# Softmax normalisation and transposes by whole query block, and the first gate/up products on 256 rows, in an attention and gated-MLP kernel

## The chip, the cores and the metric

The kernel runs on one core of one Trainium2 chip. The metric is the device time of one execution in microseconds (us); lower is better. The core has a matrix engine (TensorE, PE in the profile, whose weight loads are listed as PEld), a vector engine (VectorE, DVE), an engine for elementwise functions (ScalarE, ACT), GpSimd (POOL), and SyncE (SP), which here only issues DMAs. PSUM is the memory that PE writes to, SBUF the working memory. The engines run on their own and wait for each other by semaphores.

## The reference

`x` is 2048 rows of 512 in bf16. It is normalised by row; the result `xn` goes into a 32-head attention over given key and value caches and into a gated MLP, and the two meet in the output:

```
xn = (x - mean) / sqrt(var + 1e-5)
q  = (xn @ wq) as 32 heads of 128
p  = softmax(q k^T / sqrt(128))          # 2048 x 2048 for each head
s  = (p v, heads side by side) @ wo
h  = relu(xn @ W_gate) * (xn @ W_up)     # 1792 columns
g  = silu(h @ W_down)
out = x + s * g
```

## The kernel before

**Phases.** First comes a head (`head_ln`): layer norm of the first four 128-row tiles and their transposes. Then the MLP, in four query blocks of 512 rows (Q = 0 to 3): `emit_gate_up` computes 14 column chunks of 128 for gate and up, `emit_down` the down product. The layer norm of the later rows runs beside the first query block (`ln_task`), and their transposes are done by DMA. Then attention: 32 heads with 4 query blocks of 512 rows make 128 blocks. Then the last output tiles.

**Head.** Twelve dummy matmuls (L479) run on PE while the input loads. `ln_stats`, `ln_aggr` and `ln_coef` make mean and scale on DVE, with the square root on ACT. `ln_norm` applies them: tiles 0 and 1 on POOL, tiles 2 and 3 on DVE. `head_transpose` transposes each tile with four PE matmuls into the PSUM ring, and ACT (tiles 0 to 2) or DVE (tile 3) copies the result to `xnT`. When all four are copied, gate and up of chunk 0 begin on all 512 rows (L423, L427). The weights come in three pieces, of 2, 6 and 6 chunks; the first piece of `W_up` is loaded from ACT's queue, all others from SP's.

**Attention blocks.** A block has 8 pairs of key tiles. For each pair PE makes two score tiles of 128 keys by 512 queries (`emit_S_tile`, L583), ACT takes the exponential of both at once (L593) into one of six `PT` buffers, and three pairs later PE multiplies with the values (`emit_PV_tile`, L676): for each key tile four matmuls, one for each 128 queries, into `ps_acc`. That accumulator takes two PSUM banks with two 128-query column blocks (j) each. A value tile has a 129th column of constants, so that each column block also sums its exponentials. Score tiles and projections share a ring of three PSUM slots of two banks (`ring_acquire`).

**Between blocks.** When a block's last value product is done, DVE divides by the sums, bank by bank (`emit_norm_bank`): a reciprocal over the bank's two sums (L606), then one scaling of 128x128 for each of its column blocks (L613) into `Onorm`. The next block's first product into a bank waits for that bank's scalings. SP waits for each bank's scalings and then issues one DMA transpose per column block into `OT_store` (L628). At the first block of every group of four heads (16 blocks) DVE first waits until all transposes of the group before have landed, since the 16 `Onorm` buffers are used again.

**Filling work.** A written plan (`plan`) puts other matmuls between the last score tile of a block and the first value product of the next: the Q projection of the next head (`emit_qp`, four matmuls, L516, copied out by DVE at L527), and from block 17 on an output projection tile of the group before (`emit_oproj_tile`, L537, added up by DVE at L550). In blocks 1 to 16 there is the Q projection alone. In the last head there are no Q projections; the last output projections and the first output tiles (`emit_final_tile`, L710, L718, L723) are spread there. With group 6 DVE does two more operations per tile (`emit_base`, L562, L565).

**End.** The last block's two banks are transposed on PE (`emit_last_transposes`, `flush_last_transposes`), ACT copies them, and the last four output tiles follow; each is multiplied and added on DVE and stored by SP.

The order on each engine is the order of the program. SP's queue is in order too: a DMA behind a wait stays there until the wait ends.

## Time and profile before

| | |
|---|---|
| median of three runs | 1294.82 us (1294.73 to 1296.88) |
| profiled execution | 1294.82 us, of which the profile's span is 1293.0 us |
| PE busy | 1283.3 us, 99% |
| PE weight loads busy | 832.8 us, 64% |
| ACT busy | 1001.6 us, 77% |
| DVE busy | 442.7 us, 34% |
| granted TensorE clock | 1.00 |

A time before a row is its start in us from the span's start, then its duration. A group row gives the line, the engine, the operation, output and input tiles with partitions x elements, the count, then busy time and the mean in ns, then the idle time before it and what ended it. A row of the waits gives who waited for whom: total us, number, longest. Matmuls are pipelined, so their listed durations overlap; the distance of two starts is what one costs on PE.

### The profile page before, as it was taken

To read this page: it belongs to the slowest core of one execution; us is meant where nothing else is said; L and a number is where in the kernel's file an instruction comes from. 1 tells how busy PE (TensorE), PEld (TensorE's weight loads), DVE (VectorE), ACT (ScalarE), POOL (GpSimd) and SP (SyncE) were. 2 spreads that over 40 slices of the span, in tenths; PEclk is the share of its full clock that TensorE was granted. 3 is DMA by queue.
4 is the path that set the end of the run, shared out by engine and by line. 5 is a ranking of instruction groups with operands and counts; after the bars stand their busy time and mean duration, and the time that the engine had idled before them with its cause. 6 is when DMAs were issued, how large, how long until landed. Compare 5 with 4: busy or idle time off the path is not lost.

```text
span 1293.0 us, 27683 instructions
## 1 busy us (share of the span) xinstructions
PE 1283.3 (99%) x11968; PEld 832.8 (64%) x11968; DVE 442.7 (34%) x1190; ACT 1001.6 (77%) x1109; POOL 11.5 (1%) x23
## 2 busy tenths in 40 slices
PE   9999999999999999999999999999999999999998
PEld 4444466666666666666666666666666666666665
DVE  6333322223323323323323323323323323334456
ACT  3322399998888888888888888888888888888884
POOL 2000000000000000000000000000000000000000
PEclk9999999999999999999999999999999999999999
DMA  9500112222222322232211322222223312232202
GB/s 260 114 1 1 22 34 46 50 54 47 53 52 54 69 53 54 52 68 54 48 36 38 70 52 53 53 69 54 52 52 53 69 29 41 53 69 54 49 16 74
DMA packets 250999, 71.69 MB, mean 55 GB/s; under 512 B 237824, under 2 KB 250880, under 8 KB 250880
## 3 DMA queue, kind: packets, MB, share of 16 engines
q1 hardware_dynamic: 250064, 69.41, 25.3%
q8 instruction: 95, 1.56, 0.5%
q10 hardware_dynamic: 816, 0.52, 0.1%
q14 instruction: 24, 0.20, 0.0%
HBM read 32.77 MB, written 2.10 MB: 27 GB/s over the span
## 4 chain that ended last, share of the span: by engine, by line
PE 96%; DVE 3%; DMA 1%; issue 0%; SPq 0%; POOL 0%; ACT 0%; DVEq 0%
PE ps_acc L676 35%; PE ps_r L583 33%; PE ps_r L516 7%; PE ps_r L537 7%; PE ps_r L423 4%; PE ps_acc L460 4%; PE ps_r L427 4%; DVE Onorm L613 2%; PE ps_r L710 1%; DVE rz_sb L606 0%; DMA OT_store<-Onorm 0%; SPq L628 0%; DMA x_sb<-in_A_x_dram 0%; DVE stats L314 0%; POOL xn_sb L339 0%
## 5 line engine op out<-in xcount | busy, mean ns | idle before, releaser
L593 ACT ACTIVATE PT<-ps_r 128x1024 bf16<-128x1024 f32 x1024 | 952.5, 1053 | 173.4 <-PE ps_r L583 173.4
L676 PE MATMUL ps_acc<-V_sb,PT 128*128 128x129 bf16 x8192 | 779.8, 220 | 2.4 <-DVE Onorm L613 0.6
L676 PEld LDWEIGHTS ps_acc<-V_sb,PT 128*128 128x128 bf16 x8192 | 621.6, 98 | 246.8 <-DVE Onorm L613 5.5
L583 PE MATMUL ps_r<-QT_sb,KT_sb 128*128 128x512 bf16 x2048 | 754.1, 379 | 0.0
L606 DVE RECIPROCAL rz_sb<-ps_acc 128x2 f32<-128x2 f32 x256 | 42.3, 165 | 721.2 <-PE ps_acc L676 701.6
L583 PEld LDWEIGHTS ps_r<-QT_sb,KT_sb 128*128 128x128 bf16 x2048 | 194.9, 98 | 1.1 <-DVE QT_sb L527 0.4
L613 DVE TENSOR_SCALAR Onorm<-ps_acc,rz_sb 128x128 bf16<-128x128 f32 x512 | 156.2, 347 | 9.1
L516 PE MATMUL ps_r<-xnT,Wq_sb 128*128 128x512 bf16 x512 | 130.9, 379 | 0.0
L537 PE MATMUL ps_r<-Wo_sb,OT_store 128*128 128x512 bf16 x448 | 114.6, 379 | 0.0
L516 PEld LDWEIGHTS ps_r<-xnT,Wq_sb 128*128 128x128 bf16 x512 | 49.8, 97 | 60.7 <-ACT PT L593 27.1
L527 DVE CAST QT_sb<-ps_r 128x512 bf16<-128x512 f32 x128 | 87.2, 681 | 0.7 <-PE ps_r L516 0.7
L537 PEld LDWEIGHTS ps_r<-Wo_sb,OT_store 128*128 128x128 bf16 x448 | 43.8, 98 | 52.9 <-ACT PT L593 0.2
L433 ACT ACTIVATE gr_sb<-ps_r 128x512 bf16<-128x512 f32 x56 | 33.4, 596 | 54.3 <-PE ps_r L423 54.1
L550 DVE TENSOR_TENSOR s_acc<-s_acc,ps_r 128x512 f32<-128x512 f32 x96 | 65.9, 687 | 13.1 <-PE ps_r L537 1.0
L423 PE MATMUL ps_r<-xnT,Wg_sb 128*128 128x512 bf16 x224 | 57.5, 379 | 0.6 <-ACT xnT L357 0.6
L427 PE MATMUL ps_r<-xnT,Wu_sb 128*128 128x512 bf16 x224 | 57.5, 379 | 0.0
L439 DVE TENSOR_TENSOR hT<-gr_sb,ps_r 128x512 bf16<-128x512 bf16 x56 | 38.4, 686 | 47.8 <-PE ps_r L427 45.0
L460 PE MATMUL ps_acc<-Wd_sb,hT 128*128 128x512 bf16 x224 | 49.0, 379 | 0.0
L466 ACT ACTIVATE sig_sb<-ps_acc 128x512 f32<-128x512 f32 x16 | 9.6, 597 | 38.8 <-PE ps_acc L460 38.8
L423 PEld LDWEIGHTS ps_r<-xnT,Wg_sb 128*128 128x128 bf16 x224 | 21.9, 98 | 26.9 <-ACT xnT L357 0.7
L427 PEld LDWEIGHTS ps_r<-xnT,Wu_sb 128*128 128x128 bf16 x224 | 21.9, 98 | 26.4
L460 PEld LDWEIGHTS ps_acc<-Wd_sb,hT 128*128 128x128 bf16 x224 | 21.9, 98 | 26.4
(36 smaller groups left out, 126.8 us busy)
## 6 DMA issues: line engine op xcount, KB each, us to landing
V_sb<-in_A_v_cache_dram SPq DMA_DIRECT2D x32, 512.0 KB, 5.1
OT_store<-Onorm SPq DMA_TRANSPOSE x508, 2.4
Wq_sb<-in_A_wq_dram SPq DMA_DIRECT2D x32, 128.0 KB, 2.7
Wo_sb<-in_A_wo_dram SPq DMA_DIRECT2D x8, 512.0 KB, 4.2
Wd_sb<-in_B_W_down_dram SPq DMA_DIRECT2D x1, 1792.0 KB, 13.5
Wg_sb<-in_B_W_gate_dram SPq DMA_DIRECT2D x2, 768.0 KB, 9.0
Wu_sb<-in_B_W_up_dram SPq DMA_DIRECT2D x2, 768.0 KB, 10.0
x_sb<-in_A_x_dram SPq DMA_DIRECT2D x3, 512.0 KB, 10.8
```

Source lines behind the costliest of these rows:

```text
L423: ins = pe.matmul(ps_r[:, gb, :], Wg_sb[:, c, fs], xnT[:, c, qs], start=(c == 0), stop=(c == DC - 1))
L427: ins = pe.matmul(ps_r[:, gb + 1, :], Wu_sb[:, c, fs], xnT[:, c, qs], start=(c == 0), stop=(c == DC - 1))
L460: ins = pe.matmul(ps_acc[:, jb, 0:D], hT[par][:, fc, j * 128:(j + 1) * 128], Wd_sb[:, fc, :], start=(fc == 0), stop=(fc == FC - 1))
L516: ins = pe.matmul(ps_r[:, bank, :], Wq_sb[b][:, c, :], xnT[:, c, qs], start=(c == 0), stop=(c == DC - 1))
L527: etok = sem_qpe.sig(dve.tensor_copy(QT_sb[b][:, qs], ps_r[:, bank, :]))
L537: ins = pe.matmul(ps_r[:, bank, 0:D], OT_store[g % 2][:, hh, n * 128:(n + 1) * 128], Wo_sb[g % 2][:, hh, :], start=(hh == 0), stop=(hh == ...
L550: dve.tensor_tensor(s_acc[:, n, :], s_acc[:, n, :], ps_r[:, bank, 0:D], ALU.add)
L583: ins = pe.matmul(ps_r[:, 2 * s + tt, :], KT_sb[h % 2][:, t * 128:(t + 1) * 128], QT_sb[h % 2][:, qs], start=True, stop=True)
L593: act.activation(PT[pb][:], ps_r[:, 2 * s:2 * s + 2, :], ACTF.Exp, scale=scale)
L606: rztok = sem_rz.sig(dve.reciprocal(rz_sb[:, bank, :, :], z_ap))
L613: dve.tensor_scalar(Onorm[ob][:, j, :], ps_acc[:, bank, base:base + Dh], rz_sb[:, bank, jj, :], None, op0=ALU.mult,)
L676: ins = pe.matmul(o_ap, PT[pb][:, tt, j * 128:(j + 1) * 128], V_sb[vb][:, t, 0:VW], start=(t == 0 and j % 2 == 0), stop=(t == KT - 1 and j ...
```

## The change

1. **Normalisation by block.** `emit_norm_bank` becomes `emit_norm_block`: it waits for the whole block, then makes one reciprocal over the four sums and one multiplication of 128x512 with the reciprocals broadcast along each column block. Both accumulator banks are free when that is done. The last block keeps a two-step form, `emit_norm_last`, one multiplication of 128x256 for each half.
2. **One DMA transpose per block**, of 128x512, in place of four of 128x128. `Onorm` has 20 buffers in place of 16, and DVE's wait for the transposes of the group before moves from the group's first block to its fifth.
3. **Head.** Tiles 0 and 1 are normalised on DVE. The transposes go to the accumulator's banks in place of the ring. Gate and up of the first three chunks are made in two halves of 256 rows: the first half of chunks 0 and 1 after tiles 0 and 1, with three dummy matmuls before it; then the transposes of tiles 2 and 3, the first half of chunk 2, and the second halves. The weights come in pieces of 3, 5 and 6 chunks, and all of them from SP's queue. What follows a chunk's products is put in a function, `finish_gate_up`, and is unchanged.

The change's name also speaks of value rows at an even stride. The value tiles have a row stride of 136 elements (`VS = Dh + 8`) in both kernels, and the diff doesn't touch it.

```diff
-    NON = G * QB
+    NON = G * QB + 4
...
-    TPG = 16 * 4 * G * QB
+    TPG = 16 * G * QB
...
-                FCS = [0, min(2, FC), min(8, FC), FC]
+                FCS = [0, min(3, FC), min(8, FC), FC]
+                HFC = 3
...
-                load_w(act, Wu_sb, wu_src, sem_wu, 0)
+                load_w(sp, Wu_sb, wu_src, sem_wu, 0)
...
                 def head_transpose(n, ntok, eng, sem):
-                    tp_ps = ps_r[:, n, :].bitcast(BF16)
+                    tp_ps = acc_bf[n % 2]
+                    _wait(pe, acc_free[n % 2])
...
+                def warm_mm(k):
+                    for _i in range(k):
+                        pe.matmul(ps_r[:, 2 * NSLOT - 1, 0:D], warm[:, 0:128], warm[:], start=True, stop=True)
...
-                    n0 = ln_norm(pool, sem_nm, 0, c01)
-                    n1 = ln_norm(pool, sem_nm, 1, c01)
+                    n0 = ln_norm(dve, sem_ln4, 0, c01)
+                    n1 = ln_norm(dve, sem_ln4, 1, c01)
+                    head_transpose(0, n0, act, sem_xa)
+                    head_transpose(1, n1, act, sem_xa)
+                    warm_mm(3)
                     st = ln_stats(3)
                     sq23 = ln_aggr([2, 3], st)
+                    emit_half(0, range(HFC - 1), xt_ready[0][0:2])
                     c23 = ln_coef([2, 3], sq23)
                     n2 = ln_norm(dve, sem_ln4, 2, c23)
                     n3 = ln_norm(dve, sem_ln4, 3, c23)
-                    head_transpose(0, n0, act, sem_xa)
-                    head_transpose(1, n1, act, sem_xa)
                     head_transpose(2, n2, act, sem_xa)
                     head_transpose(3, n3, dve, sem_xt)
+                    emit_half(0, range(HFC - 1, HFC), [])
+                    emit_half(1, range(HFC), xt_ready[0][2:4])
...
+                def emit_half(k, fcs, toks):
+                    hs = slice(k * 256, (k + 1) * 256)
+                    for fc in fcs:
+                        fs = slice(fc * 128, (fc + 1) * 128)
+                        if k == 0:
+                            if fc == 0:
+                                pe.wait_ge(sem_wg[0].h, 16)
+                            half_slots.append(ring_acquire())
+                        if fc == 0:
+                            _wait_all(pe, toks)
+                        s = half_slots[fc]
+                        for i, W in enumerate((Wg_sb, Wu_sb)):
+                            if k == 0 and fc == 0 and i == 1:
+                                pe.wait_ge(sem_wu[0].h, 16)
+                            ins = None
+                            for c in range(DC):
+                                ins = pe.matmul(ps_r[:, 2 * s + i, hs], W[:, c, fs], xnT[:, c, hs],
+                                                start=(c == 0), stop=(c == DC - 1))
+                            if k == 1:
+                                half_tok[(fc, i)] = (sem_gate if i == 0 else sem_gu).sig(ins)
...
-                for _i in range(12):
-                    pe.matmul(ps_acc[:, 0, 0:D], warm[:, 0:128], warm[:], start=True, stop=True)
+                warm_mm(12)
                 head_ln()
-                ring_cnt[0] = 2
...
-                rz_sb = S_([128, 2, 2, 1], F32, "rz_sb")
+                rz_sb = S_([128, 4, 1], F32, "rz_sb")
...
-                def emit_norm_bank(b, bank, pvtok):
+                def acc_view():
+                    v = ps_acc[:].rearrange("p k (j w) -> p (k j) w", j=2)
+                    return v[:, :, 0:Dh], v[:, :, Dh:Dh + 1]
+
+                def emit_norm_block(b, pvtok):
                     h, Q = divmod(b, QB)
                     g, hh = divmod(h, G)
                     ob = b % NON
                     _wait(dve, pvtok)
-                    if bank == 0 and b % (G * QB) == 0 and g >= 1:
+                    if b % (G * QB) == 4 and g >= 1:
                         _wait(dve, t_tok(g - 1))
-                    z_ap = ps_acc[:, bank, :].rearrange("p (j w) -> p j w", j=2)[:, :, Dh:Dh + 1]
-                    rztok = sem_rz.sig(dve.reciprocal(rz_sb[:, bank, :, :], z_ap))
-                    _wait(dve, rztok)
-                    tok = None
-                    for jj in range(2):
-                        j = 2 * bank + jj
-                        base = jj * 256
-                        tok = sem_norm.sig(
-                            dve.tensor_scalar(
-                                Onorm[ob][:, j, :], ps_acc[:, bank, base:base + Dh],
-                                rz_sb[:, bank, jj, :], None, op0=ALU.mult,
-                            )
-                        )
...
+                    o_ap, z_ap = acc_view()
+                    rtok = sem_rz.sig(dve.reciprocal(rz_sb[:], z_ap))
+                    _wait(dve, rtok)
+                    tok = sem_norm.sig(
+                        dve.tensor_tensor(Onorm[ob][:], o_ap, rz_sb[:].to_broadcast([128, 4, Dh]), ALU.mult))
                     _wait(sp, tok)
...
-                    for jj in range(2):
-                        j = 2 * bank + jj
-                        tsem.sig(
-                            sp.dma_start_transpose(
-                                OT_store[g % 2][:, hh, Q * NQ + j * 128:Q * NQ + (j + 1) * 128],
-                                Onorm[ob][:, j, :],
-                            )
-                        )
+                    tsem.sig(
+                        sp.dma_start_transpose(
+                            OT_store[g % 2][:, hh, Q * NQ:(Q + 1) * NQ].rearrange("p (j q) -> p j q", j=4),
+                            Onorm[ob][:].rearrange("p j d -> p (j d)")))
+                    return tok
+
+                def emit_norm_last(b, bank, pvtok):
...
+                    o_ap, z_ap = acc_view()
+                    js = slice(2 * bank, 2 * bank + 2)
+                    rtok = sem_rz.sig(dve.reciprocal(rz_sb[:, js, :], z_ap[:, js, :]))
+                    _wait(dve, rtok)
+                    tok = sem_norm.sig(
+                        dve.tensor_tensor(Onorm[ob][:, js, :], o_ap[:, js, :],
+                                          rz_sb[:, js, :].to_broadcast([128, 2, Dh]), ALU.mult))
+                    emit_last_transposes(hh, Q, ob, bank, tok)
                     return tok
...
-                        ntx = emit_norm_bank(b, 0, tx)
-                        nty = emit_norm_bank(b, 1, ty)
-                        norm_tok[b] = (ntx, nty)
+                        if b < NBLK - 1:
+                            ntok = emit_norm_block(b, ty)
+                            norm_tok[b] = (ntok, ntok)
+                        else:
+                            emit_norm_last(b, 0, tx)
+                            emit_norm_last(b, 1, ty)
```

## The prediction

> **What bounds the kernel now.** I read the page's busy shares first, then its costliest groups, the list of waits, and the timeline around every place where TensorE (PE) or its weight loads sat idle.
>
> ```profile
> PE 1283.3 (99%) x11968; PEld 832.8 (64%) x11968; DVE 442.7 (34%) x1190; ACT 1001.6 (77%) x1109; POOL 11.5 (1%) x23
> ...
> L606 DVE RECIPROCAL rz_sb<-ps_acc 128x2 f32<-128x2 f32 x256 | 42.3, 165 | 721.2 <-PE ps_acc L676 701.6
> ...
> L613 DVE TENSOR_SCALAR Onorm<-ps_acc,rz_sb 128x128 bf16<-128x128 f32 x512 | 156.2, 347 | 9.1
> ...
> L550 DVE TENSOR_TENSOR s_acc<-s_acc,ps_r 128x512 f32<-128x512 f32 x96 | 65.9, 687 | 13.1 <-PE ps_r L537 1.0
> ```
>
> PE is the bound, so a gain can only be PE time that is waited away. The busy share hides short waits: a PV matmul is listed with 220 ns but starts come 54 to 57 ns apart, so a gap below 165 ns leaves PE "busy". Hence the waits and the distances between starts. The list of waits names the normalisation:
>
> ```profile
> DVE rz_sb L606 <- DMA OT_store<-Onorm: 19.6, 3, 6.9
> ...
> PEld ps_acc L676 <- DVE Onorm L613: 5.5, 18, 0.5
> ```
>
> One early block boundary in the timeline:
>
> ```profile
> 167.16 0.39 PE L676 MATMUL ps_acc<-V_sb,PT 128*128 128x129 bf16 x4
> ...
> 167.47 0.17 DVE L606 RECIPROCAL rz_sb<-ps_acc 128x2 f32<-128x2 f32 x1 [6.02 <-PE ps_acc L676]
> 167.68 0.61 DVE L613 TENSOR_SCALAR Onorm<-ps_acc,rz_sb 128x128 bf16<-128x128 f32 x2
> ...
> 167.82 1.03 PE L516 MATMUL ps_r<-xnT,Wq_sb 128*128 128x512 bf16 x4
> 168.20 0.16 DVE L606 RECIPROCAL rz_sb<-ps_acc 128x2 f32<-128x2 f32 x1
> ...
> 168.40 0.61 DVE L613 TENSOR_SCALAR Onorm<-ps_acc,rz_sb 128x128 bf16<-128x128 f32 x2
> ...
> 168.68 0.90 PE L676 MATMUL ps_acc<-V_sb,PT 128*128 128x129 bf16 x8
> ...
> 169.06 0.34 PEld L676 LDWEIGHTS ps_acc<-V_sb,PT 128*128 128x128 bf16 x6 [0.28 <-DVE Onorm L613]
> ```
>
> Bank 1's normalisation ends at 169.02, 1.47 us after the block's last matmul (167.55), while PE has only two score matmuls and one Q projection to do. In blocks 1 to 16 nothing else covers it: their reciprocals come 8.225 us apart. Full blocks, with an output projection of 4 x 0.216 = 0.864 us more, come 8.807 apart and show no wait. So 8.225 - (8.807 - 0.864) = 0.28 us are lost, 16 times. Two group boundaries and one block of the last head add to it, and the head of the program shows when work begins:
>
> ```profile
> 581.93 0.17 DVE L606 RECIPROCAL rz_sb<-ps_acc 128x2 f32<-128x2 f32 x1 [6.87 <-DMA OT_store<-Onorm]
> ...
> 583.52 0.51 PE L676 MATMUL ps_acc<-V_sb,PT 128*128 128x129 bf16 x6 [0.27 <-DVE Onorm L613]
> ```
>
> ```profile
> 1254.36 0.51 PE L676 MATMUL ps_acc<-V_sb,PT 128*128 128x129 bf16 x6 [0.35 <-DVE Onorm L613]
> ```
>
> ```profile
> 1.19 5.30 PE L479 MATMUL ps_acc<-warm 128*128 128x512 bf16 x12 [1.19 <-DVE warm L234]
> ...
> 6.07 1.52 POOL L339 TENSOR_SCALAR xn_sb<-x_sb,rstd,nmr 128x512 bf16<-128x512 bf16 x2 [4.39 <-DVE nmr L333]
> ...
> 6.98 0.38 PE L351 MATMUL ps_r<-ident,xn_sb 128*128 128x128 bf16 x4 [0.49 <-POOL xn_sb L339]
> ...
> 7.40 1.75 ACT L357 COPY xnT<-ps_r 128x512 bf16<-128x512 bf16 x3 [0.23 <-PE ps_r L351]
> ...
> 9.38 1.02 PE L423 MATMUL ps_r<-xnT,Wg_sb 128*128 128x512 bf16 x4 [0.56 <-ACT xnT L357]
> ```
>
> **The change part by part.** The profiled execution took 1294.82 us (span 1293.0 and 1.8 around it), which is the median of the three runs; the sum is made against it.
>
> *Whole-block normalisation, early blocks.* Removed: two reciprocals and four 128x128 scalings per block. Added: one reciprocal over 4 columns and one TENSOR_TENSOR of 128x512 with the reciprocal broadcast. No row shows a broadcast operand. Bounds: 0.68 us (the Q cast L527, same size, one operand) and 1.37 (twice L550, if the broadcast halved the rate); I take L550's 0.69, the same operation with an f32 PSUM operand and the same size. It now waits for all four column blocks: 167.55 + 0.04 (167.43 to 167.47 before), + 0.21 reciprocal with its gap (167.47 to 167.68), + 0.69, + 0.04 to the waiting load (169.02 to 169.06) = 168.53. Both banks wait for this now, where bank 0 was free at 168.29. PE's earliest PV matmul is 168.68, set by four projections of 0.216 from 167.82, and a load can precede its matmul by as little as 0.03 (1253.70 and 1253.73 in the timeline). So there are 0.12 us to spare, and the stall goes: 16 x 0.28 = -4.5. What is late next? ACT: its eight exponentials take 7.44 us of a block of 7.94, so it stays off the path. In full blocks the slack is 0.98.
>
> *One transpose per block, Onorm four buffers longer, the wait moved.* SP issues 127 transposes in place of 508. The nearest row is the head's xnT transpose of the same 128x512: 1.19 to 1.87 us to issue and 2.5 to landing, against 4 x 1.23 us. At 573 to 582 four issues queued behind a V load hold DVE (L606's wait for DMA). At blocks 48 and 64 this costs PE 18.06 - 17.61 = 0.45 and 17.76 - 17.61 = 0.15 us over two blocks; the other boundaries cost nothing. DVE now asks four blocks later, over 26 us after the issue. -0.6. Behind SP's wait for the norm stand the K, V and Wq loads; they come earlier or stay, and no PE wait names them.
>
> *Block 124.* DVE is late there by three oproj operations and reaches the reciprocal at 1252.77; bank 1's matmuls begin about 0.54 us after their place. New: 1252.97 + 0.69 + 0.04 = 1253.70, and PE is ready at 1253.73. -0.5.
>
> *Tail.* From 1280.94 to the end DVE works through two half-block norms and eight final tiles of 1.06 us. Each norm goes from a 0.73 us step to 0.2 + 0.42 - 0.08 = 0.54 (0.42 is L550 less 256 of its 512 elements, at the 1.04 ns per element that L550 and the 128-wide rows give). -0.35; PE's first final tile is done at 1281.88, before DVE asks at 1282.02.
>
> *Head.* DVE normalises tiles 0 and 1 (0.41 each, as n2, n3 show) in place of POOL (0.77 each): ready at 6.42 and 6.76. Transposes from 6.49, ACT copies (0.58 each) to 8.07, gate/up on 256 rows from about 8.2 instead of 9.38. No row has a 256-column matmul; PV's 129 columns at 57 ns and 512 at 216 put it between 0.108 (half) and 0.11, so 16 take 1.73: to 9.93. Stats of tile 3 wait behind the two norms, and the square root of tiles 2, 3 stands in ACT's queue behind the second copy (8.07): those norms end at 9.22 and 9.55, before PE's transposes at 9.93, which take 0.43. Third chunk to 11.2, copies done 11.0, second halves 24 x 0.108 to 13.8; before, three chunks were done at 9.38 + 6 x 0.864 = 14.56. That is -0.75. The first W_up now queues behind W_gate on SP: 1.28 MB have to pass, which the stretches of the first 10 us reach at about 6.3 us; W_gate landed some 1.5 us after its bytes, so 7.8, against need at 8.6. The next pieces: about 11.3 against 13.8. ReLU and product of chunk 0 free their slot at 13.24, before 13.8. Three dummy matmuls fit in while ACT copies. The unknown is PE's pace: the twelve dummies start 0.43 us apart, the transposes at 6.98 0.053 apart; the new transposes fall between. Bounds -0.75 and -0.45 (T0 at 0.107 a piece, and its copy later); I take -0.65.
>
> Here a rule speaks against the change. The Trainium skill, "TensorE: Matmul & The Clock Gate", section "What's actually happening", says that the half-rate clock ends after a busy window of some 3.4 us of a free-running counter, so that the moment differs by run. By it a run whose switch falls late would lose the 0.3 us named, and the head would give 0.45 and the total 1288.4; in this trace the switch fell between 5.9 and 6.98 us.
>
> *Value stride.* Both kernels hold VS = 136; nothing changes, 0.
>
> Sum: -4.5 - 0.6 - 0.5 - 0.35 - 0.65 = -6.6; 1294.8 - 6.6 = **1288.2 us**.
>
> **Rivals.**
> 1. *The broadcast product is slow (slower).* Place: the 17 boundaries with one cover item. Beyond 0.69 + 0.12 = 0.81 us each tenth costs 1.7 us. At 1.37: 17 x 0.56 = 9.5 in place of the 5.0 lost now, while the other boundaries stay covered up to 1.67: -6.6 + 9.5 = +2.9, 1297.7. It decides from 0.81 + 6.6/17 = 1.20. Against: L439, L550 and L718 all take 0.68 to 0.69 with one PSUM operand, whatever the other one's type. For: none has a zero stride.
> 2. *It only partly fits.* At 0.90 to 1.14 (four scalings back to back, 0.347 + 3 x 0.265): 1.5 to 5.6 given back, 1289.7 to 1293.8.
> 3. *The head gives nothing*: W_up at 8.9 or later, or copies slower than half a tile's share: 1288.9.
> 4. *The change doesn't remove the wait*, another releaser standing behind it (a ring slot held by ACT): 16 x 0.28 stay, 1292.7. Against: PE runs gapless before and after the wait, and ACT restarts only after it.
>
> **How the numbers follow.** Forecast 0.64, rival 3 0.12, rival 2 0.12, rival 1 0.08, rival 4 0.04. A difference under 0.2% (2.6 us) can't be told from none. Faster: 0.64 + 0.12 + 0.09 of rival 2, and 0.01 of 4 = 0.86; same: 0.06, out of rivals 2, 4 and 1 below 1.35 us; slower 0.08. Low end 1287.0: the head at 0.75, the tail at 0.37 and a us for the spread that two of the three runs don't show; high end 1291.8, which takes in rival 3 and most of rival 2.
>
> **What would show it.** Right: reciprocals of early blocks 7.94 us apart; one TENSOR_TENSOR of about 690 ns per block; no idle weight load before PV at 169 to 293; no DVE wait for OT_store; 127 transposes; first 256-row matmul at 8.2 and the fourth chunk at 13.8. Wrong: that product above 0.8 us, gaps in the halves (weights or copies late), or a granted clock below 1.00.

## The result, and the profile after

The changed kernel takes 1287.97 us (1287.70 to 1288.06); the kernel before, run beside it, 1294.78 us. The ratio is 0.9943, 95% interval 0.9926 to 0.9961. The forecast was 1288.2. The profiled execution took 1287.70 us, with a span of 1285.8 and a granted clock of 0.999; before it was 1294.82 and 1293.0.

The page of the profile after, with the busy shares and the two groups of the normalisation (busy time and mean in ns behind the bar):

```profile
PE 1279.2 (99%) x11995; PEld 834.8 (65%) x11995; DVE 380.0 (30%) x682; ACT 1001.4 (78%) x1109; POOL 10.0 (1%) x21
...
L652 DVE RECIPROCAL rz_sb<-ps_acc 128x4 f32<-128x4 f32 x127 | 23.3, 183 | 729.6 <-PE ps_acc L722 729.6
...
L655 DVE TENSOR_TENSOR Onorm<-ps_acc,rz_sb 128x512 bf16<-128x512 f32 x127 | 87.8, 691 | 4.4
```

The product with the broadcast reciprocal takes 691 ns, which is what the same operation takes without a broadcast (687 ns at L550 before). DVE has 508 instructions fewer (1190 to 682) and 63 us less to do, but DVE wasn't the bound, and that saving by itself is worth nothing. What counts is in the list of waits after (who waited for whom, total us, number, longest):

```profile
DVE rz_sb L652 <- PE ps_acc L722: 729.6, 126, 6.1
...
PEld ps_acc L722 <- ACT PT L635: 3.5, 13, 0.4
```

Neither the wait for `OT_store` (19.6 us in 3 waits) nor the one of the value products' weight loads for `Onorm` (5.5 us in 18) is left. The weight loads now name ACT, and those entries cost PE nothing, as the timeline of an early block boundary after shows:

```profile
166.08 0.39 PE L722 MATMUL ps_acc<-V_sb,PT 128*128 128x129 bf16 x4
...
166.30 0.59 PE L625 MATMUL ps_r<-QT_sb,KT_sb 128*128 128x512 bf16 x2
166.50 0.18 DVE L652 RECIPROCAL rz_sb<-ps_acc 128x4 f32<-128x4 f32 x1 [6.13 <-PE ps_acc L722]
...
166.72 0.69 DVE L655 TENSOR_TENSOR Onorm<-ps_acc,rz_sb 128x512 bf16<-128x512 f32 x1
166.74 1.03 PE L558 MATMUL ps_r<-xnT,Wq_sb 128*128 128x512 bf16 x4
...
167.53 0.51 PEld L722 LDWEIGHTS ps_acc<-V_sb,PT 128*128 128x128 bf16 x8 [0.26 <-ACT PT L635]
167.60 0.62 PE L722 MATMUL ps_acc<-V_sb,PT 128*128 128x129 bf16 x8
```

The four projections start at 166.74 and take 4 x 0.216 = 0.864, so PE is ready at 167.60, and at 167.60 the value products start. DVE's product ended at 167.41. The load's idle time of 0.26 us lies under the projections: the load starts 0.12 us after DVE's product ends, and PE isn't ready before 167.60. From here to block 17 the reciprocals come 7.94 us apart (8.225 before).

The head in the timeline after:

```profile
1.19 4.25 PE L365 MATMUL ps_r<-warm 128*128 128x512 bf16 x12 [1.19 <-DVE warm L235]
...
5.60 0.74 DVE L340 TENSOR_SCALAR xn_sb<-x_sb,rstd,nmr 128x512 bf16<-128x512 bf16 x2
...
6.16 0.63 PE L353 MATMUL ps_acc<-ident,xn_sb 128*128 128x128 bf16 x8 [0.71 <-DVE xn_sb L340]
...
6.58 1.07 ACT L359 COPY xnT<-ps_acc 128x512 bf16<-128x512 bf16 x2 [1.53 <-PE ps_acc L353]
...
7.80 0.60 PE L407 MATMUL ps_r<-xnT,Wg_sb 128*128 128x256 bf16 x4 [0.36 <-ACT xnT L359]
...
13.48 1.03 PE L481 MATMUL ps_r<-xnT,Wg_sb 128*128 128x512 bf16 x4
```

Two tiles are copied at 7.65 and the first half matmul starts at 7.80, where before all four had to be copied, by 9.38. PE then has enough work of 256 rows for tiles 2 and 3 to be ready in time, and the fourth chunk starts at 13.48 (14.56 before).

**Where the time went.** The same event was read off both profiles; its shift grows from stage to stage:

| stage | gain, us | forecast, us |
|---|---|---|
| head, to the start of the fourth chunk | 1.08 | 0.65 |
| the sixteen early blocks | 4.53 | 4.5 |
| boundaries of the groups of heads | 0.59 | 0.6 |
| block 124 | 0.44 | 0.5 |
| block 126, one wait of an output projection for its ring slot | 0.17 | none |
| tail | 0.36 | 0.35 |
| sum (span 1293.0 to 1285.8) | 7.17 | 6.6 |

Two of these rows hold a share that belongs to the execution and not to the change. The statistics of the first tile of x begin when its load lands: at 3.56 us in the profile before, at 3.15 in the one after, and anywhere from 3.14 to 3.75 in the fourteen profiles of this study. The head's gain without that is 1.08 - 0.41 = 0.67. And the 0.17 us at block 126 stand in the profile before alone: there blocks 125 and 126 are 10.71 us apart; after, and in three kernels below that keep the old normalisation, it is 10.53. Without the two, 6.59 us remain.

To compare single profiles, I use two figures for each kernel: the start of the fourth chunk and the end of the span, both less the start of the first tile's statistics (x lands). Spans are taken to 0.01 us. Where the first matmul of the fourth chunk is missing in a trace, the fifth chunk less 1.73 us stands for it.

| kernel | median, us | x lands | fourth chunk after it | span after it |
|---|---|---|---|---|
| before | 1294.78 | 3.56 | 11.00 | 1289.44 |
| after | 1287.97 | 3.15 | 10.33 | 1282.67 |
| head_only | 1294.19 | 3.38 | 10.32 | 1288.42 |
| norm_only | 1288.74 | 3.25 | 11.42 | 1283.73 |
| prod_twice | 1297.58 | 3.25 | 10.63 | 1292.46 |
| four_scalings | 1294.69 | 3.40 | 10.32 | 1289.39 |
| late_wait | 1294.06 | 3.36 | 11.01 | 1288.70 |
| one_transpose | 1294.03 | 3.33 | 11.00 | 1288.69 |
| four_transposes | 1288.53 | 3.53 | 10.37 | 1283.46 |
| no_halves | 1289.88 | 3.52 | 12.13 | 1284.46 |
| pool_norms | 1288.59 | 3.14 | 10.93 | 1283.27 |
| wu_act | 1289.06 | 3.31 | 11.52 | 1283.85 |
| no_dummies | 1288.71 | 3.53 | 10.33 | 1282.64 |
| tail | 1288.14 | 3.75 | 10.32 | 1282.85 |

The kernel before scatters more than the changed one (1294.43 to 1297.9 over all its runs), and its median beside the experiments lay between 1294.8 and 1296.1; the differences below are therefore read from the table's last column and from the timelines, and the ratios are given with their intervals. The changed kernel was not run again beside the experiments.

### The profile page after: what moved, and what is told of

Its sections match the earlier page's. It is cut to its first block, busy times and chain, and to the rows that moved or that the text cites. A ratio compares the mean times of both kernels' runs of the same rounds, so it can differ in the third digit from the quotient of the medians.

```text
span 1285.8 us, 26847 instructions
## 1 busy us (share of the span) xinstructions
PE 1279.2 (99%) x11995; PEld 834.8 (65%) x11995; DVE 380.0 (30%) x682; ACT 1001.4 (78%) x1109; POOL 10.0 (1%) x21
## 4 chain that ended last, share of the span: by engine, by line
PE 99%; DVE 1%; issue 0%; DMA 0%; ACT 0%
PE ps_acc L722 36%; PE ps_r L625 34%; PE ps_r L558 9%; PE ps_r L579 8%; PE ps_acc L504 4%; PE ps_r L485 4%; PE ps_r L481 4%; PE ps_r L759 1%; DVE fin_tmp L767 0%; PE ps_r L407 0%; DMA x_sb<-in_A_x_dram 0%; DVE stats L315 0%; ACT xnT L359 0%; PE ps_acc L353 0%; DVE x_sb L772 0%
## 5 line engine op out<-in xcount | busy, mean ns | idle before, releaser
L652 DVE RECIPROCAL rz_sb<-ps_acc 128x4 f32<-128x4 f32 x127 | 23.3, 183 | 729.6 <-PE ps_acc L722 729.6
L655 DVE TENSOR_TENSOR Onorm<-ps_acc,rz_sb 128x512 bf16<-128x512 f32 x127 | 87.8, 691 | 4.4
L485 PE MATMUL ps_r<-xnT,Wu_sb 128*128 128x512 bf16 x212 | 54.4, 379 | 0.0
L481 PE MATMUL ps_r<-xnT,Wg_sb 128*128 128x512 bf16 x212 | 54.4, 379 | 0.0
```

Source lines behind the costliest of these rows:

```text
L481: ins = pe.matmul(ps_r[:, gb, :], Wg_sb[:, c, fs], xnT[:, c, qs], start=(c == 0), stop=(c == DC - 1))
L485: ins = pe.matmul(ps_r[:, gb + 1, :], Wu_sb[:, c, fs], xnT[:, c, qs], start=(c == 0), stop=(c == DC - 1))
L655: dve.tensor_tensor(Onorm[ob][:], o_ap, rz_sb[:].to_broadcast([128, 4, Dh]), ALU.mult))
```

## The experiments

### The two halves of the change

`head_only` has the new head and the old attention; `norm_only` the reverse.

```
 head_only: after, with
-    NON = G * QB + 4
+    NON = G * QB
-    TPG = 16 * G * QB
+    TPG = 16 * 4 * G * QB
 ...
 and emit_norm_bank with its two calls per block, as before

 norm_only: before, with
-    NON = G * QB
+    NON = G * QB + 4
-    TPG = 16 * 4 * G * QB
+    TPG = 16 * G * QB
 ...
 and emit_norm_block, emit_norm_last with their calls, as after
```

> The new head with the old attention part (bank-wise normalisation, four transposes per block, 16 Onorm buffers). My account, read off the two traces: the head is worth what chunk 3 starts earlier, 14.56 to 13.48 us in the profiled executions, and nothing of it is given back later, so about 1293.7 us, with the 16 waits of 0.28 us still there. The forecast had 0.65 us for it (1294.1). Rival: the lead is eaten before attention starts (a ring slot or the weights), 1294.8. Second rival: the head carries most of the gain, below 1290.

> The old head with the new attention part. My account: 4.5 for the 16 early boundaries, 0.6 for the two group boundaries, 0.5 for block 124, 0.2 for a ring wait two blocks later and 0.35 in the tail make 6.1, so 1288.7 us, and the first gate matmul stays at 9.4 us. Rival (the gain comes from the head): above 1293.

`head_only`: 1294.19 us (1293.67 to 1294.82), ratio 0.9987 (0.9978 to 0.9996). The fourth chunk comes 10.32 us after x, as after; early blocks are 8.225 apart, as before. The span after x is 1.02 us shorter than before: 0.68 in the head, 0.17 at block 126, and 0.16 because the wait for `OT_store` costs 0.43 in this execution, at block 16, in place of 0.59 at blocks 48 and 64.

`norm_only`: 1288.74 us (1288.34 to 1288.81), ratio 0.9943 (0.9931 to 0.9956). Early blocks are 7.94 apart, no wait for `OT_store`. Its span after x is 1.06 above that of after, and the head alone is 1.09 later (11.42 against 10.33). The old head is 11.00 elsewhere; here DVE waited another 0.29 us for the third tile of x, in front of the scale of tiles 0 and 1.

The two parts therefore add up, and nearly all of the gain is the normalisation's.

### What the broadcast product may cost

The forecast rests on 0.12 us of spare time at each early boundary. `prod_twice` makes the product a second time, into a buffer that nobody reads; `four_scalings` makes the whole-block reciprocal, but then the four old scalings.

```
 prod_twice
+                    _wait(dve, scr_tok[0])
+                    scr_tok[0] = sem_norm.sig(
+                        dve.tensor_tensor(scr[:], o_ap, rz_sb[:].to_broadcast([128, 4, Dh]), ALU.mult))
                     tok = sem_norm.sig(
                         dve.tensor_tensor(Onorm[ob][:], o_ap, rz_sb[:].to_broadcast([128, 4, Dh]), ALU.mult))

 four_scalings
-                    tok = sem_norm.sig(
-                        dve.tensor_tensor(Onorm[ob][:], o_ap, rz_sb[:].to_broadcast([128, 4, Dh]), ALU.mult))
+                    for j in range(4):
+                        tok = sem_norm.sig(
+                            dve.tensor_scalar(
+                                Onorm[ob][:, j, :], ps_acc[:, j // 2, (j % 2) * 256:(j % 2) * 256 + Dh],
+                                rz_sb[:, j, :], None, op0=ALU.mult,
+                            )
+                        )
```

> The changed kernel with the block's broadcast multiplication made twice, first into a scratch tile, so that it costs 1.37 us in place of 0.69. The forecast's limit: the 17 boundaries with a single projection have 0.12 us to spare, so each loses 0.55 to 0.65 us and the full blocks lose nothing: plus 9.5 to 11, 1297.5 to 1299, reciprocals of the early blocks about 8.5 us apart and those of the full blocks still 8.81. Rival: the boundary is held by something else (ACT or a ring slot) and the product has more room: below 1292. Second rival: full blocks are near their limit too: over 1310.

> The changed kernel with one reciprocal per block, but four 128x128 scalings in place of the one broadcast multiplication; both banks still wait for all four. Four scalings take 0.347 + 3 x 0.265 = 1.14 us, 0.45 more than the multiplication. With 0.04 to 0.12 us to spare that is 0.33 to 0.41 at each of 17 boundaries: 1293.6 to 1295 us, nearly the kernel before. Rival: waiting once per block is what pays, not the single multiplication: 1288 to 1290.

`prod_twice`: 1297.58 us (1297.37 to 1299.54), ratio 1.0012 (1.0003 to 1.0021). Early reciprocals are 8.50 apart in place of 7.94; full blocks stay at 8.81. An early boundary in its timeline:

```profile
175.41 0.18 DVE L654 RECIPROCAL rz_sb<-ps_acc 128x4 f32<-128x4 f32 x1 [6.39 <-PE ps_acc L727]
...
175.63 0.69 DVE L658 TENSOR_TENSOR scr<-ps_acc,rz_sb 128x512 bf16<-128x512 f32 x1
175.64 1.03 PE L560 MATMUL ps_r<-xnT,Wq_sb 128*128 128x512 bf16 x4
176.23 0.68 DVE L660 TENSOR_TENSOR Onorm<-ps_acc,rz_sb 128x512 bf16<-128x512 f32 x1
...
177.06 0.61 PE L727 MATMUL ps_acc<-V_sb,PT 128*128 128x129 bf16 x8 [0.39 <-DVE Onorm L660]
```

The second product ends 0.60 us after the first (back to back, a product costs less than its listed 0.69), and the value products start at 177.06 in place of 175.64 + 0.864 = 176.50: 0.56 late. So 0.04 us were to spare, not 0.12. The two rows next to the wait say the same: here, where PE does wait, its first value product starts 0.15 us after DVE's product ends (176.91 to 177.06); in the profile after it is 0.19 (167.41 to 167.60).

Sixteen times 0.554, 0.63 at block 124 and 0.30 in the head make 9.79, by which the span after x is longer. The share of the head has nothing to do with the product. It belongs to this execution:

```profile
6.28 0.72 PE L353 MATMUL ps_acc<-ident,xn_sb 128*128 128x128 bf16 x8
...
8.04 0.60 PE L407 MATMUL ps_r<-xnT,Wg_sb 128*128 128x256 bf16 x4 [0.38 <-ACT xnT L359]
...
8.62 0.33 PEld L407 LDWEIGHTS ps_r<-xnT,Wu_sb 128*128 128x128 bf16 x4 [0.27 <-DMA Wu_sb<-in_B_W_up_dram]
```

The first two transposes start 0.107 us apart here, and 0.055 in the profile after; the first half matmul comes 4.79 us after x in place of 4.64, 0.14 later. The other 0.16 are a wait for `W_up`.

`four_scalings`: 1294.69 us (1294.52 to 1295.04), ratio 0.9992 (0.9983 to 1.0001). Early reciprocals are 8.337 apart; a boundary in its timeline:

```profile
175.30 1.13 DVE L656 TENSOR_SCALAR Onorm<-ps_acc,rz_sb 128x128 bf16<-128x128 f32 x4
175.32 1.03 PE L558 MATMUL ps_r<-xnT,Wq_sb 128*128 128x512 bf16 x4
...
176.58 0.61 PE L727 MATMUL ps_acc<-V_sb,PT 128*128 128x129 bf16 x8 [0.23 <-DVE Onorm L656]
```

Four scalings back to back take 1.13, 0.44 more than the product; the boundary grows by 0.394. That again leaves 0.04 of spare. So it is the single instruction that pays. Making one reciprocal for the block and waiting for the whole block, with the scalings left as four, is a loss: the early blocks are then longer than before (8.337 against 8.225), since bank 0 no longer gets its turn early. The limit at which rival 1 begins to cost anything is 0.69 + 0.04 = 0.73 us a product, not 0.81.

### The transposes and the moved wait

The change does two things here at once. `late_wait` is the kernel before with 20 `Onorm` buffers and the wait at the group's fifth block; `one_transpose` is the kernel before with one transpose per block, and the old buffers and wait; `four_transposes` is after, with four transposes, 16 buffers and the old wait.

```
 late_wait (before)
-    NON = G * QB
+    NON = G * QB + 4
-                    if bank == 0 and b % (G * QB) == 0 and g >= 1:
+                    if bank == 0 and b % (G * QB) == 4 and g >= 1:
                         _wait(dve, t_tok(g - 1))

 one_transpose (before)
-    TPG = 16 * 4 * G * QB
+    TPG = 16 * G * QB
 ...
+                    if bank == 0:
+                        return tok
 ...
-                    for jj in range(2):
 ...
+                    tsem.sig(
+                        sp.dma_start_transpose(
+                            OT_store[g % 2][:, hh, Q * NQ:(Q + 1) * NQ].rearrange("p (j q) -> p j q", j=4),
+                            Onorm[ob][:].rearrange("p j d -> p (j d)")))

 four_transposes (after)
-    NON = G * QB + 4
+    NON = G * QB
 ...
-                    if b % (G * QB) == 4 and g >= 1:
+                    if b % (G * QB) == 0 and g >= 1:
 ...
-                    tsem.sig(
 ...
+                    for j in range(4):
+                        tsem.sig(
+                            sp.dma_start_transpose(
+                                OT_store[g % 2][:, hh, Q * NQ + j * 128:Q * NQ + (j + 1) * 128],
+                                Onorm[ob][:, j, :],
+                            )
+                        )
```

> The kernel before with only the buffers and the wait changed: 20 Onorm buffers, DVE asks for the transposes of the group before at the group's fifth block; four transposes per block and the bank-wise normalisation stay. Account: the wait of DVE for OT_store goes, with it what it costs PE at the group boundaries, 0.6 us in the profile of before (blocks 48 and 64); the 16 early waits of 0.28 stay: 1294.2 us by the profile. The kernel before has so far spread over 1294.6 to 1297.9 us while the kernels without that wait spread over 0.5: if the wait is the cause of the spread, this one stays within 1 us and near 1294.2. Rival: the number of DMAs is what counts, and the wait or a stall elsewhere remains: as before, with its spread.

> The kernel before with only the transposes changed: one of 128x512 per block, issued after the second bank's scalings; 16 Onorm buffers and DVE's wait at the group's first block stay. Account: one issue in place of four lands some 5 us earlier, before DVE asks, so the wait goes just as with the later question: 1294.2 us, spread within 1 us. Rival: landing of that one transpose is later, behind the K, V and Wq loads of the next head, and the wait remains at some of the seven boundaries: 1294.8 or more.

> The kernel after with four transposes of 128x128 per block, sixteen Onorm buffers and the wait for the old transposes at the first block of a group, as in the kernel before; the head, the whole-block normalisation and the tail are those of after. The forecast put -0.6 us on this part; the later tests showed that either one transpose or the later wait alone clears the wait at blocks 48 and 64. So: DVE waits for OT_store again, blocks 48 and 64 cost 0.45 and 0.15 us more, 1288.6. Rival: with two DVE instructions per block in place of six, and the chain 0.5 us shorter, the wait is there but covered: 1288.0.

`late_wait`: 1294.06 us (1293.62 to 1296.53), ratio 0.9995 (0.9986 to 1.0004). `one_transpose`: 1294.03 us (1293.81 to 1295.79), ratio 0.9994 (0.9985 to 1.0002). By the ratios alone neither can be told from no change. The profiles do tell: DVE's wait for `OT_store` is gone in both, all distances of full blocks are 8.81, and the spans after x are 0.74 and 0.75 shorter than before, of which 0.17 is block 126 and 0.59 the boundaries. Either half is enough, since each alone removes the same wait.

What fell is an idea that I had by then, that this wait is what makes the times of the kernel before scatter: both kernels are without it, and still four or five of their eleven times lie some 2 us above the rest, with a mean granted clock of 0.998 where the others have 0.999 or 1.000. None of these was profiled, so the cause stays open.

`four_transposes`: 1288.53 us (1288.36 to 1288.89), ratio 0.9941 (0.9928 to 0.9955). The wait for `OT_store` is back, and the span after x is 0.79 longer than after's. The size is near the expected 0.6, the place isn't: at blocks 32, 48 and 112 DVE comes up to 0.40 us late and nothing follows from it, since two blocks together are 17.61 us, as without a wait. 0.77 of the loss lies at block 16, here in the timeline of `four_transposes`:

```profile
286.08 0.18 DVE L652 RECIPROCAL rz_sb<-ps_acc 128x4 f32<-128x4 f32 x1 [5.96 <-PE ps_acc L725]
...
294.25 1.03 PE L558 MATMUL ps_r<-xnT,Wq_sb 128*128 128x512 bf16 x4
295.64 0.55 PEld L579 LDWEIGHTS ps_r<-Wo_sb,OT_store 128*128 128x128 bf16 x4 [0.86 <-DMA OT_store<-Onorm]
295.65 1.04 PE L579 MATMUL ps_r<-Wo_sb,OT_store 128*128 128x512 bf16 x4 [0.37 <-DMA OT_store<-Onorm]
295.69 0.18 DVE L652 RECIPROCAL rz_sb<-ps_acc 128x4 f32<-128x4 f32 x1 [7.63 <-DMA OT_store<-Onorm]
295.91 0.69 DVE L655 TENSOR_TENSOR Onorm<-ps_acc,rz_sb 128x512 bf16<-128x512 f32 x1
...
296.75 0.61 PE L725 MATMUL ps_acc<-V_sb,PT 128*128 128x129 bf16 x8
```

Two instructions need these transposes: DVE's reciprocal, whose buffers must be free, and PE's first output projection of group 0. PE was ready for the projection at 294.25 + 0.864 = 295.11 and starts it at 295.65, 0.54 late. It would then have reached the value products at 296.51; the late normalisation makes that 296.75, another 0.24. In the profile after neither waits. So this part of the change guards two readers, and where it costs something differs by execution: DVE's wait at blocks 48 and 64 before and at block 16 in `head_only`, both waits at block 16 here.

### The four steps of the head

Each of these is after with one step undone.

```
 no_halves
-                HFC = 3
+                HFC = 0
 ...
-                    emit_half(0, range(HFC - 1), xt_ready[0][0:2])
 ...
-                    emit_half(0, range(HFC - 1, HFC), [])
-                    emit_half(1, range(HFC), xt_ready[0][2:4])

 pool_norms
-                    n0 = ln_norm(dve, sem_ln4, 0, c01)
-                    n1 = ln_norm(dve, sem_ln4, 1, c01)
+                    n0 = ln_norm(pool, sem_nm, 0, c01)
+                    n1 = ln_norm(pool, sem_nm, 1, c01)

 wu_act
-                load_w(sp, Wu_sb, wu_src, sem_wu, 0)
+                load_w(act, Wu_sb, wu_src, sem_wu, 0)

 no_dummies
-                    warm_mm(3)
```

> The changed kernel without the 256-row halves: tiles 0 and 1 still on DVE, weights in pieces of 3, 5, 6 on SP, three dummies, but gate and up of every chunk on 512 rows, after all four copies. Account: with PE free the transposes of tiles 2 and 3 come at about 9.0, the copies end at about 9.9 and chunk 3 starts 5.18 us later at 15.1, 1.0 to 1.6 us after the changed kernel's 13.5 to 14.1: 1289 to 1289.6 us, worse than the old head. Rival (the gain comes from the norms on DVE): 13.5 to 14.1 again, 1288.

> The changed kernel with tiles 0 and 1 normalised on POOL as before (0.77 us each in place of 0.41). Account: the second tile is ready 0.75 us later, the gate opens at 8.3 to 8.6 in place of 7.8 to 8.05, while the statistics of tile 3 come 0.8 us earlier and hide behind the first halves: chunk 3 0.4 to 0.6 us later, 1288.4 to 1288.6 us. Rival: the opening is set by the weights and not by the tiles: 7.8 to 8.05 again.

> The kernel after with the first piece of W_up issued from ACT's queue again, as the kernel before does, in place of SP's. My account of the move to SP: it orders the bytes, so that tile 0 of x and W_gate come before W_up. Undone, x's first tile lands up to 0.4 us later and W_gate later by part of W_up's time, 1288.2 to 1288.5 us, with the statistics of tile 0 starting at 3.5 in place of 3.15 us. Rival: the order of two queues of the same sixteen engines changes nothing that PE waits for: 1288.0, and the start of the statistics lies within what it is in the other kernels (3.14 to 3.56).

> The kernel after without the three dummy matmuls that stand between the head's first transposes and its first half of gate/up. My account: PE idles there in any case while ACT copies the transposed tiles (6.8 to 7.8 us in the profile after), so nothing moves: 1288.0 us, first half matmul at 7.8 to 8.4 and the fourth chunk at 13.5 to 14.1. Rival: the dummies are what keeps PE at its full rate until the first half; without them the twelve first dummies may end before the rate has changed, and the first half of gate/up runs at half rate: 8 matmuls of 256 columns at 0.22 in place of 0.11 us, 0.9 us later, 1288.9, or a second group of times 1.5 to 2 us above the others, as the kernel before has it.

`no_halves`: 1289.88 us (1289.77 to 1291.64), ratio 0.9963 (0.9949 to 0.9976). Gate starts at 10.47 on 512 rows and the fourth chunk 12.13 us after x, 1.13 later than with the old head; its timeline:

```profile
6.52 0.63 PE L353 MATMUL ps_acc<-ident,xn_sb 128*128 128x128 bf16 x8 [0.27 <-DVE xn_sb L340]
...
9.20 0.71 PE L353 MATMUL ps_acc<-ident,xn_sb 128*128 128x128 bf16 x8 [1.40 <-DVE xn_sb L340]
...
10.47 0.81 PE L478 MATMUL ps_r<-xnT,Wg_sb 128*128 128x512 bf16 x3 [0.56 <-ACT xnT L359]
```

Tiles 0 and 1 on DVE delay the statistics of tile 3, and the transposes of tiles 2 and 3 come at 9.20. Without halves that delay stands on the path; with them it lies under the first half. The norms on DVE are a gain only together with the halves.

`pool_norms`: 1288.59 us (1288.30 to 1288.70), ratio 0.9949 (0.9936 to 0.9963); the fourth chunk comes 10.93 us after x, 0.60 later than after. POOL needs 1.52 us for the two tiles, DVE 0.74.

`wu_act`: 1289.06 us (1288.11 to 1289.57), ratio 0.9944 (0.9930 to 0.9958); the fourth chunk comes 11.52 us after x, 1.19 later than after and 0.52 later than before. One of the four runs, 1288.11 us with a span of 1286.2, is nearly as short as the changed kernel's, so the loss isn't in every execution. In the profiled one it is more than the 0.2 to 0.5 expected, and comes through another transfer than the one moved, as the timeline shows:

```profile
9.12 0.28 PE L407 MATMUL ps_r<-xnT,Wg_sb 128*128 128x256 bf16 x1 [1.37 <-DMA Wg_sb<-in_B_W_gate_dram]
```

It is `W_gate` that is late: it lands 7.4 us after its issue, 4.6 in the profile after and 4.4 to 5.5 in all nine profiles with both loads in SP's queue. `W_up`, issued beside it from ACT's queue, lands 7.9 us after its own issue. That the two hold each other up fits this, but isn't shown: in the four kernels with the old head, whose first pieces of 256 KB also go out from two queues, `W_gate` lands 4.4 to 5.6 us after its issue. In one queue `W_gate` comes first, and `W_up` in time but for 0.16 us in `prod_twice`. The landing of x, at 3.31, lies within what the other profiles have.

`no_dummies`: 1288.71 us (1288.16 to 1288.76), ratio 0.9941 (0.9929 to 0.9954). Fourth chunk 10.33 and end 1282.64 us after x, as after (10.33 and 1282.67); x landed 0.38 later in this execution. The three dummy matmuls do nothing that can be seen in the span: the half matmuls are 0.109 us apart without them too. The median is 0.74 us above the changed kernel's all the same, but not by the span, whose median is 1286.2 against 1286.1: in four of the five runs 2.5 to 2.7 us of the time lie outside the span, 1.8 to 1.9 in the changed kernel's. No run shows what that is.

### A shorter tail

After the last score tile DVE works without a gap to the end, 1.06 us a tile. This kernel gives the add of every second tile of the last eight to POOL and puts the last block's transposes in front of two tiles instead of between.

```
+                    if n >= NT - 8 and n % 2 == 0:
+                        _wait(pool, mtok)
+                        ftok = sem_nm.sig(
+                            pool.tensor_tensor(x_sb[:, n, :], x_sb[:, n, :], fin_tmp[fb][:], ALU.add))
 ...
-                for n in range(NT - 8, NT - 4, 2):
-                    emit_M([(emit_final_tile, n), (emit_final_tile, n + 1)])
+                emit_M([(emit_final_tile, NT - 8), (emit_final_tile, NT - 7)])
                 flush_last_transposes()
+                emit_M([(emit_final_tile, NT - 6), (emit_final_tile, NT - 5)])
```

> An attempt at a faster kernel than after: for the last eight tiles the final add of the even tiles goes from DVE to POOL, and the transposes of the last block stand before the third and fourth of these tiles, so that PE doesn't wait between them. In the profile after DVE works from 1275.21 to the end at 1.06 us a tile, 0.34 of it the add that shows between two products. Four adds less on DVE: 4 x 0.34 = 1.4 us at most; PE's eight final tiles of 0.905 us, from 1274.04, with 0.4 for the transposes, end at 1281.7, and product and add follow to 1282.9, against 1283.8: -0.7 to -1.4, 1286.6 to 1287.3. Rival: POOL's add takes more than two tiles' time (over 2 us), or slows DVE's own work beside it, and the outputs of the pairs come later: 1288.0 or above.

1288.14 us (1288.02 to 1288.52), ratio 0.9938 (0.9924 to 0.9951): no better than after, by the rival's second reason. Its timeline:

```profile
1277.93 1.40 DVE L767 TENSOR_TENSOR fin_tmp<-ps_r,g_sb 128x512 bf16<-128x512 f32 x2
1278.69 1.16 POOL L774 TENSOR_TENSOR x_sb<-x_sb,fin_tmp 128x512 bf16<-128x512 bf16 x1 [0.96 <-DVE fin_tmp L767]
1279.37 0.75 DVE L779 TENSOR_TENSOR x_sb<-x_sb,fin_tmp 128x512 bf16<-128x512 bf16 x1
1280.05 1.40 DVE L767 TENSOR_TENSOR fin_tmp<-ps_r,g_sb 128x512 bf16<-128x512 f32 x2
```

DVE's own add takes 0.75 in place of 0.43 us, and ends 0.27 us after POOL's add (1280.12 and 1279.85), as the other three do within 0.01, whenever they began. Two tiles take 2.12 us, exactly twice 1.06. The products beside POOL's add, with one operand in PSUM, keep their length. The Trainium skill has a rule for this ("SBUF — State Buffer", section "Who interferes with whom"): an instruction of VectorE with two SBUF inputs meets GpSimd's reads at a shared port, and one of the two waits for the whole of the other. These rows agree that the add with two SBUF inputs is held by POOL's add and the product with one isn't; but an add of 0.43 us that ends 0.27 after POOL's was not held as a whole. The other half of the edit, PE without its wait between the tiles, does what it says, but PE is not what the tail waits for.

## Why the prediction was right

**Early blocks.** Right in mechanism and size: 16 x 0.283 = 4.53, and `norm_only` shows it without the head. The step "0.12 us to spare" was wrong by two thirds: it was 0.04. Two terms of the chain were too short: the reciprocal with its gap (0.22 in place of 0.21) and above all the step from the product's end to the load, taken as 0.04 and 0.12 in the profile after (167.41 to 167.53). The result holds since any spare time above zero gives the same gain. But I argued with a cushion of 0.12 us when I gave the partial rival its chance; a product slower by a tenth would have cost time. That it fits was luck in part.

**The unknown row.** The broadcast was taken at 0.69 us from L550, between 0.68 and 1.37. It measured 0.691. The upper end had no row that spoke for it.

**Transposes and wait.** 0.6 forecast, 0.59 in the two profiles, 0.77 in `four_transposes`. The forecast had the wait at blocks 48 and 64 and DVE as the only one hurt. The place changes from execution to execution and the first projection of a group can be hurt too, so the profile before showed one draw of a varying cost.

**Block 124.** 0.5 forecast, 0.44 measured. The forecast had the load free at 1253.70 and PE ready at 1253.73. After, the product ends at 1247.48, the load starts at 1247.60 and the matmul at 1247.63, where 1246.67 + 0.864 = 1247.53 was to be had. These and the tail's rows in the timeline after:

```profile
1246.67 1.03 PE L579 MATMUL ps_r<-Wo_sb,OT_store 128*128 128x512 bf16 x4
1246.79 0.69 DVE L655 TENSOR_TENSOR Onorm<-ps_acc,rz_sb 128x512 bf16<-128x512 f32 x1
...
1247.60 0.47 PEld L722 LDWEIGHTS ps_acc<-V_sb,PT 128*128 128x128 bf16 x8 [0.39 <-ACT PT L635]
1247.63 0.61 PE L722 MATMUL ps_acc<-V_sb,PT 128*128 128x129 bf16 x8
...
1274.13 0.17 DVE L673 RECIPROCAL rz_sb<-ps_acc 128x2 f32<-128x2 f32 x1 [0.35 <-PE ps_acc L722]
...
1275.21 0.68 DVE L767 TENSOR_TENSOR fin_tmp<-ps_r,g_sb 128x512 bf16<-128x512 f32 x1
```

The load's row names ACT for the idle time, but ACT had been done; what came last is DVE's product, 0.12 us ahead. It is the same step of 0.12 as above, and 0.1 us of stall is left.

**Tail.** The two half norms take 1275.21 - 1274.13 = 1.08 us, 2 x 0.54 as forecast, and the end comes 0.36 sooner (forecast 0.35). The 0.42 for a product of 128x256 was met, but not for the reason given: L550 and the 128-wide L613 give (687 - 347)/384 = 0.89 ns per element, not 1.04, and by that the product would have been 0.46. After, 691 ns for 512 elements and 0.42 us for 256 make 1.06.

**Head.** 0.65 forecast, 0.67 measured once the landing of x is taken out, and 0.68 in `head_only`. The steps were right too: with 0.41 us for x added, the gate opens at 8.20 (forecast 8.2), the second transposes come at 9.94 (9.93) and the fourth chunk at 13.88 (13.8). The range given, 0.45 to 0.75, was for the pace of PE; the larger uncertainty was one that I didn't name, that x lands anywhere in 0.6 us. It may also be why the profiled gain, 7.17, is larger than the 6.8 between the medians, whose runs weren't all profiled. The rule on the clock that was weighed against the head came out in part. The twelve dummies took 4.08 to 5.30 us over the profiles; in `tail` their starts go from 0.43 to 0.22 us apart after the seventh, in seven profiles not before the twelfth, so the moment at which PE gets its full rate does vary by run. A late one cost 0.14 us in `prod_twice` and 0.04 in `four_transposes`, where the first transposes still ran at the lower rate; the 0.3 us named appeared in none (in `wu_act` the wait for `W_gate` hides whatever it cost).

**Rivals.** The broadcast isn't slow (1), it fits, if barely (2), the head gives its part (3), and no other releaser stood behind the wait (4). `four_scalings` shows what rival 2 would have brought at its upper end: 1294.69, where 1293.8 was given; the overrated cushion, 17 x 0.08 = 1.3, accounts for that. `prod_twice` is rival 1 with a product of 0.60 + 0.69 = 1.29 us: by the forecast's own working -6.6 + 17 x (1.29 - 0.81) = +1.6, 1296.4; it took 1297.58, for the same reason and the 0.30 in the head.

**The name's third part**, the even stride of the value rows, is in both kernels and costs and brings nothing here.

**The sum.** That the time agrees to 0.2 us is luck in part. The sum went from an execution of 1294.82 us, while the times of the kernel before lie between 1294.43 and 1297.9; what the runs tested are the terms.

## What to carry to other kernels

A vector chain between two matmul groups is worth shortening only where the matmuls that cover it are few: read the distance between starts in covered and uncovered blocks, and the difference times the number of uncovered ones is the gain. When the chain then just fits, measure the slack by adding a known instruction to it, since a slack worked out from rows of the kernel before was off by two thirds here. And take the moment at which the first load lands out of both profiles before comparing two of them, when the question is about a microsecond.

## What the runs showed of the hardware

- A DVE multiplication of 128x512 from PSUM with a second operand broadcast at stride zero takes 691 ns, the same as with a full operand (687 ns); issued back to back, it costs 0.60 us.
- A matmul that waits for a DVE product starts 0.15 us after the product's listed end, and the weight load before it 0.12 after, at all sixteen early boundaries of `prod_twice` and of `four_scalings`.
- Four DVE scalings of 128x128 back to back take 1.13 us, where one multiplication of the same 512 columns takes 0.69.
- A DMA transpose of 128x512 from `Onorm` takes 1.19 us of SP's queue and 2.4 us to land (medians after), the same as one of 128x128 (1.23 and 2.4, before).
- A DVE add of two SBUF operands beside a POOL add of the same kind ends 0.27 us after that one and takes 0.75 us in place of 0.43; a DVE multiplication with one PSUM operand keeps its 0.69.
- Two loads of 384 KB issued from two queues both came late in the one profile that has them: `W_gate` landed 7.4 us after its issue beside `W_up` from ACT's queue, and 4.4 to 5.5 us with `W_up` behind it in SP's.
- The load of x's first tile, 128 KB, is issued at 0.74 us, and the statistics that wait for it start between 3.14 and 3.75 us over fourteen executions.
